# Attention and a wide layer on one core: small products of the identity in the gaps that the planner sees on TensorE

## The chip, the cores and the metric

The kernel runs on one core of one Trainium2 chip. The metric is the device time of one execution in microseconds; less is better. Three runs of the kernel before took 984.73 to 985.93 us, with a median of 985.3 us.

## What is computed

The inputs are q, k and v of shape 8 x 8 x 576 x 64 (batch, heads, positions, head dimension), two weights of 512 x 2048 and 2048 x 512, all float32. The first part is causal attention in a window of 128 positions with a linear bias per head; the second part is a layer on its output, taken as 4608 tokens of 512:

```python
scores = where(0 <= i - j < 128, q @ k.T / 8 - slope[head] * abs(i - j), -1e9)
x = softmax(scores) @ v                      # heads side by side: 4608 x 512
h = x @ w_in
g = h * erf(log1p(exp(h)))
out = g @ w_out
```

## The kernel before, in words

The attention goes in 48 steps of two heads each (`Attention`). A step makes scores on TensorE (L543 for the first eight steps, L614 later), adds the bias on VectorE (L648), takes exponentials on ScalarE (L656), scales by the sums on GpSimd (L679), turns the result (for the first eight steps on TensorE with the identity, L567, copied out by ScalarE or VectorE at L514 and L518; later on VectorE, L696) and multiplies by the values on TensorE (L589, L718). The sums are copied out of PSUM by ScalarE and VectorE (L762, L763, L514, L518).

The layer goes in two passes over the hidden dimension, 7 blocks of 128 and then 9 (`Moe.one_pass`). Each weight and each activation is split into a high and a low part, so each product becomes three. A unit is one block of hidden rows by 384 tokens (512 in the second pass): two halves of six products each (L926, `unit`, one planner operation for each half), a copy of the sums to `hs` by ScalarE (L908) or VectorE (L912), softplus and erf on ScalarE (L963, L965), products and splits on VectorE (L975, L979) and ScalarE, and the products with the second weight (L997). The first pass runs beside the attention. There all units share one PSUM bank for their sums, bank 3 ("h", one buffer): the next unit's first half waits for the copy of the last unit. Columns 0 to 383 hold the sums. The first two attention steps use the whole bank for their turned blocks. In the second pass the units' sums lie in four other banks and are 512 columns wide; a unit whose sums fall into two `hs` buffers is copied in two pieces of 256 columns, each a planner operation of its own that either engine may take.

The weights are read by DMA, put together from two words and split by ScalarE, GpSimd and VectorE (`Weights.prepare`, L802 to L823).

A list scheduler sets the order of the work (`Plan`, L205 on). Every operation has a cost per engine and a due time; `run` (L263) goes through time and gives each engine the ready operation with the earliest due time. It has its own model of TensorE's clock (`on_pe`, L293) and of the delay from one engine to another (`hop`, L219, for example 0.08 + 0.14 + 0.6 = 0.82 us from ScalarE to TensorE). The result is the list `order`, in the order of the decisions; the loop at L366 emits each operation in this order, and each engine runs its own instructions in it. The waits between engines are set from what each emitted instruction reads and writes; all eight banks are one tile, `banks` (L200).

Before the first scores the kernel runs products of a block of zeros (`warm_up`, L478, L485): 22 products of 128 x 128, with the latest due time, so that the planner puts them where TensorE has nothing else to do.

Of the kernel before, what the change touches and what calls it, by code (L numbers as in the profile page):

```python
# [34 lines left out]
ROWS = 0.5  # L35
PLAIN, EARLY = 8, 2
DIRECT = 4
WARM = 22
AHEAD, VA = 4, 13
ND = 3  # L40
# [14 lines left out]
MC, MP, MH = 0.01, 16, -20  # L55
# [155 lines left out]
class Plan:  # L211
# [17 lines left out]
    def op(self, costs, emit, r=(), w=(), at=0.0, moved=0, rows=1.0):  # L229
        o = Op()  # L230
        o.rows = rows
        o.costs, o.emit, o.at, o.seq, o.moved, o.lag = costs, emit, at, len(self.ops), moved, 0.0
        o.outs, o.start, o.engine = [], None, None
        deps, bufs = set(), {}
        for b in r:
            if b.writer:
                deps.add(b.writer)
            b.readers.append(o)
            bufs[id(b)] = b
        for b in w:  # L240
            if b.writer:
                deps.add(b.writer)
            deps.update(b.readers)
            b.writer, b.readers = o, []
            bufs[id(b)] = b
        for b in r:
            if b.writer is o:
                b.readers = []
        for b in [*r, *w]:
            if isinstance(b, Part):  # L250
                bufs[id(b.whole)] = b.whole
        deps.discard(o)
        o.deps, o.bufs = deps, list(bufs.values())
        for b in o.bufs:
            b.users += 1
            if b.users == 1 and b.tag is not None:
                self.slots.setdefault((id(b.pool), b.tag), [b.bufs, []])[1].append(b)
        for d in deps:
            d.outs.append(o)
        self.ops.append(o)  # L260
        return o

    def run(self):  # L263
# [3 lines left out]
        free = {}  # L267
# [51 lines left out]
        while events:  # L319
# [3 lines left out]
            while done and done[0][0] <= t + 1e-9:  # L323
                _, _, o = heapq.heappop(done)
# [38 lines left out]
                    heapq.heappush(events, best.end + best.lag)  # L363
        assert len(order) == len(self.ops), (len(order), len(self.ops))
        self.time = max(o.end for o in order)
        for o in order:  # L366
            self.emit(o)

    def emit(self, o):
# [3 lines left out]
def f32r_us(n):  # L373
    return max(n / 2400.0 + 0.0135, 0.11)
# [6 lines left out]
def dve(n, fast=False):  # L381
    return 0.1 + n * (0.00054 if fast else 0.00108)


def act(n, aps=0, src=0.11):
    return src + 0.093 * aps + n * 0.00084
# [18 lines left out]
def step_time(n):  # L405
    return TE * min(n, NE) + TA * max(0, n - NE)
# [21 lines left out]
class Attention:  # L428
# [49 lines left out]
    def warm_up(self):  # L478
# [4 lines left out]
        op({"DVE": dve(P)}, lambda e: nc.vector.memset(x[:, :P], 0.0), w=[x], at=-30)  # L483
        for _ in range(WARM):
            op({"PE": 0.215}, lambda e: nc.tensor.matmul(  # L485
# [265 lines left out]
    def apply(self, y):  # L751
# [3 lines left out]
        n, c, g, px, at = y.n, y.c, y.g, y.px, y.at + LT  # L755
        if c < DIRECT:
            xs = Part(self.moe.direct(c), slice(None), g, slice(0, CH))
# [70 lines left out]
class Moe:  # L828
# [85 lines left out]
    def unit(self, c, f, w, x, po, start, end, at):  # L914
        nc, op, W = self.nc, self.plan.op, self.width
        U = self.U
        wh, wl = w.t[0, f]
        ps = Buf(self.h_home[0], [P, 512], F32, *self.h_home[1:], f"h{U}")
        for k2 in range(2):
            xh, xl = x[k2]  # L920

            def products(e, k2=k2, xh=xh, xl=xl):
                for k in range(2):
                    cs = slice((2 * k2 + k) * P, (2 * k2 + k + 1) * P)
                    for n, (ww, xx) in enumerate(((wh, xh), (wh, xl), (wl, xh))):
                        nc.tensor.matmul(  # L926
                            ps[:, :W], lhsT=ww[:, cs], rhs=xx[:, k],
                            start=(k2 + k + n == 0), stop=(k2 + k + n == 4),
                        )

            op({"PE": 6 * f32r_us(W) + 0.015}, products, r=[wh, wl, xh, xl], w=[ps], at=at + MH)
        if not self.round:
            self.hs = []
        pos, end_ = len(self.round) * W, (len(self.round) + 1) * W
        base = pos
        while pos < end_:
            i, off = divmod(pos, MW)
            n = min(MW - off, end_ - pos)
            if not off:
                self.hs.append(Buf(self.hp, [P, MW], F32, "m", MB, f"hs{U}_{i}", keep=KH))  # L940
            hs = self.hs[i]
            op({"Act": act(n, src=0.06), "DVE": dve(n)},
               lambda e, hs=hs, off=off, n=n, p0=pos - base: self.copy(e, hs[:, off : off + n], ps[:, p0 : p0 + n]),
               r=[ps], w=[hs], at=at)
            pos += n
        return dict(U=U, c=c, f=f, w=w, po=po, start=start, end=end, at=at)
# [82 lines left out]
@with_exitstack  # L1029
def tile_kernel(ctx, tc, qk, vb, w_in, w_out, plain, bias, out, nb=B):  # L1030
    nc = tc.nc
    nt = nb * S
    nch = nt // CH
    ctx.enter_context(tc.manual_schedule())
    dram = ctx.enter_context(tc.tile_pool(name="dram", bufs=1, space=DRAM))
    const = ctx.enter_context(tc.tile_pool(name="const", bufs=1))
    ident = const.tile([P, P], F32, name="ident")
    nc.scalar.preload_act_table_set(LOG_EXP_SET)
    make_identity(nc, ident)
    x_dram = [Buf(ap=dram.tile([P, NK, CH], F32, name=f"xd{c}")) for c in range(nch)]  # L1040
    part = [Buf(ap=dram.tile([P, DM], F32, name=f"pd{t}")) for t in range(nt // P)]
    plan = Plan()
    w1p = ctx.enter_context(tc.tile_pool(name="w1p", bufs=1))
    stage = ctx.enter_context(tc.tile_pool(name="stage", bufs=1))
    moe = Moe(tc, plan, ctx, x_dram, part, out)
    actx = ctx.enter_context(ExitStack())
    attention = Attention(tc, plan, actx, qk, vb, plain, bias, ident, moe)
    ops = list(plan.ops)


    n1 = nch * NF1
    t0 = LEAD
    t1 = t0 + n1 * TM
    w1 = Weights(nc, plan, lambda k, f: (w1p, f"{k}_{f}"), stage, w_in, w_out, range(NF1), attention.loaded[3:4])
    for k in range(2):
        for f in range(NF1):
            w1.prepare(k, f, t0 - W1A + (f * W1C + W1B * k) * TM)
    accs = [(moe.ps, f"o{t}") for t in range(CH // P)]
    moe.h_home = moe.ps, "h", 1
    moe.one_pass(w1, True, CH, accs, lambda U: t0 + U * TM)  # L1060


    gone, w2p = Buf(ap=True), []

    def close(e):
        actx.close()
        w2p.append(ctx.enter_context(tc.tile_pool(name="w2p", bufs=1)))

    ops += [o for o in plan.ops[len(ops) :] if any(b in o.bufs for b in (moe.raw[1], moe.raw[2]))]
    plan.op({"SP": 0.0}, close, w=[gone], at=0.0).deps.update(ops)  # L1070
    last = plan.ops[-1]
    for o in ops:
        o.outs.append(last)
    pool2 = lambda: w2p[0]
    place = lambda k, f: (
        (pool2, f"{k}_{f}") if f < NF1 + FIT else (w1p, f"{k}_{f - NF1 - FIT}")
    )
    w2 = Weights(nc, plan, place, stage, w_in, w_out, range(NF1, NF))
    tw = step_time(9 * NPAIR * nb // 2)
    for k in range(2):  # L1080
        for f in range(NF1, NF):
            w2.prepare(k, f, tw - W2A + (f - NF1 + (NF - NF1) * k) * W2B, after=[gone])
    moe.h_home = moe.ps, "s", 4
    moe.one_pass(w2, False, CH2, [*accs, (moe.ps, "h")], lambda U: t1 + (U - n1) * TN, pool2, [gone])
    plan.run()
    return plan

# [72 lines left out]
```

## Time and profile before

| | us |
|---|---|
| median of 3 runs (lowest, highest) | 985.3 (984.73, 985.93) |
| the profiled execution | 985.25 |
| its span | 983.3 |
| TensorE busy | 955.2 |
| ScalarE busy | 608.3 |
| VectorE busy | 561.1 |
| GpSimd busy | 149.3 |

The profile is of one execution. Its times are microseconds from the start of the span. PE is TensorE's matmuls, PEld its weight loads, DVE is VectorE, ACT is ScalarE, POOL is GpSimd and SP is SyncE, which issues DMAs. L926 is line 926 of the kernel. A row of instructions names what is written and read (`banks<-xh,whi`). An idle time before an instruction is put down to the work that ended it. The granted clock is the share of TensorE's full clock that the chip granted in a stretch.

### The profile page before, as it was taken

The numbers are of one execution on the slowest core, as the hardware profiler recorded it, in microseconds if no ns is written. First come the engines' busy times: TensorE is split into PE (matmuls) and PEld (weight loads), VectorE is DVE, ScalarE is ACT, GpSimd is POOL, SyncE is SP. The second block draws the span as 40 slices with busy tenths as digits, with TensorE's granted clock in tenths as the row PEclk, the third lists the DMA queues.
The fourth block names the chain that finished last, engine by engine and source line by source line (L and its number), as shares of the span: only waits on it lengthen the run. The fifth ranks groups of instructions, "written<-read, shape, count | busy, mean of one in ns | idle before, by whom it ended". The sixth has DMA issues, their size and how long they took to land.

```text
span 983.3 us, 25856 instructions
## 1 busy us (share of the span) xinstructions
PE 955.2 (97%) x10936; PEld 801.7 (82%) x10936; DVE 561.1 (57%) x1336; ACT 608.3 (62%) x1245; POOL 149.3 (15%) x297
## 2 busy tenths in 40 slices
PE   8788999999999999999999999999999999999997
PEld 6577877888888888989998888888888888888886
DVE  6877885776667666774389434343434343434342
ACT  7878885678667865786688563636363636363552
POOL 3444333333233323000001000000000000000000
PEclk9988999999999999999999999999999999999999
DMA  6675555547555552551034112121212121212021
GB/s 232 217 220 178 171 188 169 184 144 226 180 165 171 184 192 87 199 168 37 33 116 142 64 43 86 43 86 43 87 43 86 43 86 43 86 43 86 1 65 43
DMA packets 52932, 115.09 MB, mean 117 GB/s; under 512 B 5584, under 2 KB 22736, under 8 KB 52816
## 3 DMA queue, kind: packets, MB, share of 16 engines
q1 hardware_dynamic: 52816, 113.43, 36.1%
q8 instruction: 86, 1.41, 0.6%
q14 instruction: 30, 0.25, 0.1%
HBM read 85.10 MB, written 28.31 MB: 115 GB/s over the span
## 4 chain that ended last, share of the span: by engine, by line
PE 81%; ACT 6%; DVE 4%; POOL 3%; DMA 3%; issue 2%; SPq 0%; ACTq 0%; POOLq 0%; DVEq 0%
PE banks L997 37%; PE banks L926 36%; PE banks L718 5%; POOL p L679 3%; PE banks L614 3%; DMA wri<-w_in 2%; ACT p L656 1%; DVE pa L696 1%; ACT s L963 1%; DMA tables<-bias 1%; ACT s L965 1%; ACT L965 1%; ACT L963 1%; ACT L967 0%; ACT wui L809 0%
## 5 line engine op out<-in xcount | busy, mean ns | idle before, releaser
L926 PE MATMUL banks<-xh,whi 128*128 128x384 f32 (+1 forms) x660 | 245.6, 372 | 8.2 <-ACT hs L908 5.5
L926 PE MATMUL banks<-xh,wli 128*128 128x384 f32 (+1 forms) x660 | 240.9, 365 | 1.3 <-DVE wli L823 1.3
L926 PE MATMUL banks<-xl,whi 128*128 128x384 f32 (+1 forms) x660 | 240.7, 365 | 0.0
L997 PE MATMUL banks<-who,gh 128*128 128x512 f32 x576 | 229.6, 399 | 0.5 <-DVE ot L912 0.5
L997 PE MATMUL banks<-wlo,gh 128*128 128x512 f32 x576 | 225.3, 391 | 0.3 <-issue 0.3
L997 PE MATMUL banks<-who,gl 128*128 128x512 f32 x576 | 225.4, 391 | 0.0
L908 ACT COPY hs<-banks 128x384 f32<-128x384 f32 (+2 forms) x127 | 58.4, 468 | 224.0 <-PE banks L926 223.9
L679 POOL TENSOR_SCALAR p<-p,st 128x160 f32<-128x160 f32 (+2 forms) x282 | 139.0, 514 | 228.1 <-DVE st L671 175.4
L926 PEld LDWEIGHTS banks<-xh,whi 128*128 128x128 f32 x660 | 125.1, 190 | 31.1 <-ACT hs L908 7.7
L912 DVE COPY hs<-banks 128x512 f32<-128x512 f32 (+2 forms) x66 | 37.8, 573 | 190.1 <-PE banks L926 170.2
L926 PEld LDWEIGHTS banks<-xl,whi 128*128 128x128 f32 x660 | 125.4, 190 | 15.5
L926 PEld LDWEIGHTS banks<-xh,wli 128*128 128x128 f32 x660 | 125.1, 190 | 14.1 <-DVE wli L823 1.7
L656 ACT ACTIVATE p<-p,st 128x160 f32<-128x160 f32 (+2 forms) x288 | 120.5, 423 | 25.1 <-DVE st L648 23.5
L997 PEld LDWEIGHTS banks<-who,gh 128*128 128x128 f32 x576 | 108.1, 188 | 27.7 <-issue 6.3
L997 PEld LDWEIGHTS banks<-who,gl 128*128 128x128 f32 x576 | 108.1, 188 | 23.5 <-DVE hs L975 0.5
L997 PEld LDWEIGHTS banks<-wlo,gh 128*128 128x128 f32 x576 | 108.1, 188 | 19.3
L975 DVE TENSOR_TENSOR hs<-s,hs 128x768 f32<-128x768 f32 (+1 forms) x106 | 89.9, 884 | 17.3 <-ACT s L965 17.3
L648 DVE CUSTOM_DVE_ANT_0 p<-banks,tables 128x160 f32<-128x160 f32 (+2 forms) x288 | 75.3, 319 | 31.3 <-PE banks L614 30.8
L979 DVE TENSOR_TENSOR gl<-hs,gh 128x768 fp32r<-128x768 f32 (+1 forms) x106 | 91.0, 888 | 0.7
L963 ACT ACTIVATE s<-hs 128x768 f32<-128x768 f32 (+1 forms) x106 | 76.5, 776 | 0.5
L965 ACT ACTIVATE s<-s 128x768 f32<-128x768 f32 (+1 forms) x106 | 76.4, 776 | 0.5
L718 PEld LDWEIGHTS banks<-pa,v 32*64 32x64 f32 x4576 | 59.5, 132 | 14.5 <-issue 8.6
(66 smaller groups left out, 874.5 us busy)
## 6 DMA issues: line engine op xcount, KB each, us to landing
v<-v_b SPq DMA_DIRECT2D x24, 512.0 KB, 4.0
xr<-xd SPq DMA_DIRECT2D x14, 768.0 KB, 4.9
qk<-qk SPq DMA_DIRECT2D x24, 400.0 KB, 4.1
pd<-ot SPq DMA_DIRECT2D x36, 256.0 KB, 3.8
ot<-pd SPq DMA_DIRECT2D x36, 256.0 KB, 3.4
wri<-w_in SPq DMA_DIRECT2D x16, 512.0 KB, 4.2
qk<-qk SPq DMA_DIRECT2D x16, 512.0 KB, 4.6
wro<-w_out SPq DMA_DIRECT2D x16, 512.0 KB, 4.1
```

The source lines that it names most:

```text
L648: nc.vector.tensor_tensor_reduce(out=dst(j), in0=cut(ps[j].all), in1=cut(table[:, half * j + c0 : half * j + c0 + n]), scale=-0.125, scala ...
L656: nc.scalar.activation(dst(j), dst(j), AF.Exp, bias=low[:, j : j + 1], scale=-1.0, accum_out=total[:, j : j + 1])
L679: (nc.vector if e == "DVE" else nc.gpsimd).tensor_scalar(dst, dst, totals[t][:, j : j + 1], 1.0, op0=ALU.mult, op1=ALU.mult)
L718: nc.tensor.matmul(whole[64 * j : 64 * j + 64, first + a, 32 * t0 : 32 * (t0 + n)], lhsT=y.v[rows, 128 * slot + 64 * j : 128 * slot + 64 * ...
L908: self.nc.scalar.copy(out, src)
L912: self.nc.vector.tensor_copy(out, src)
L926: nc.tensor.matmul(ps[:, :W], lhsT=ww[:, cs], rhs=xx[:, k], start=(k2 + k + n == 0), stop=(k2 + k + n == 4),)
L963: A.activation(s[:, :n], hs[:, :n], AF.Softplus)
L965: A.activation(s[:, :n], s[:, :n], AF.Erf)
L975: op({"DVE": dve(n)}, lambda e, s=s, hs=hs, n=n: V.tensor_tensor(hs[:, :n], s[:, :n], hs[:, :n], ALU.mult), r=[s, hs], w=[hs], at=at)
L979: op({"DVE": dve(n)}, lambda e, gh=gh, gl=gl, hs=hs, n=n: V.tensor_tensor(gl[:, :n], hs[:, :n], gh[:, :n], SUB), r=[hs, gh], w=[gl], at=at)
L997: nc.tensor.matmul(po.all, lhsT=gg[:, cs], rhs=w.all, start=(u["start"] and n == 0), stop=(u["end"] and n == 2),)
```

## The change

The planner's loop that emits the operations looks at those of TensorE. If an operation's start in the list lies between 26 and 110 us, if it starts more than 0.3 us after the end of TensorE's operation before it, and if no unit is half done, it first emits int(gap / 0.22) products of the identity with itself, 128 x 128, into columns 384 to 511 of bank 3. A unit is half done between its two halves: the first half's operation is marked open, the second one's not open. Nothing reads those columns in the first pass. The order of all other operations stays as it was.

```diff
+REST = 26, 110
...
         self.time = max(o.end for o in order)
+        free, half = 0.0, False
         for o in order:
+            if o.engine == "PE":
+                if not half and REST[0] < o.start < REST[1] and o.start - free > 0.3:
+                    self.rest(int((o.start - free) / 0.22))
+                free = o.end
+                half = o.open if hasattr(o, "open") else half
             self.emit(o)
...
-            op({"PE": 6 * f32r_us(W) + 0.015}, products, r=[wh, wl, xh, xl], w=[ps], at=at + MH)
+            op({"PE": 6 * f32r_us(W) + 0.015}, products, r=[wh, wl, xh, xl], w=[ps], at=at + MH).open = not k2
...
+    def rest(count):
+        for _ in range(count):
+            nc.tensor.matmul(moe.ps.whole[:, 3, 384:], lhsT=ident[:, :], rhs=ident[:, :], start=True, stop=True)
+
+    plan.rest = rest
     plan.run()
```

## Rows read from the trace of the kernel before

**Rows 1.** The page: the busy time of TensorE with its share and instructions, the granted clock in 40 equal slices of the span (tenths, 9 is 90% or more), and the shares of the chain of waits by engine.
```profile
PE 955.2 (97%) x10936; PEld 801.7 (82%) x10936; DVE 561.1 (57%) x1336; ACT 608.3 (62%) x1245; POOL 149.3 (15%) x297
...
PEclk9988999999999999999999999999999999999999
...
PE 81%; ACT 6%; DVE 4%; POOL 3%; DMA 3%; issue 2%; SPq 0%; ACTq 0%; POOLq 0%; DVEq 0%
```
**Rows 2.** The windows of the trace: for each stretch its start and end, its length, the busy time of TensorE, its weight loads, VectorE, ScalarE and GpSimd, each with its count, then the granted clock, the share of the DMA engines and GB/s.
```profile
31.20:34.90 3.70, 3.28 (x54) 2.94 (x54) 2.12 (x6) 1.21 (x4) 0.76 (x2) 0.55 0.72 268
48.80:55.80 7.00, 6.88 (x89) 5.18 (x90) 4.74 (x17) 4.82 (x15) 4.02 (x8) 0.53 0.63 202
62.20:65.70 3.50, 3.19 (x10) 3.19 (x11) 3.33 (x7) 1.51 (x3) 1.82 (x3) 0.51 0.69 248
79.40:86.10 6.70, 6.09 (x123) 5.59 (x124) 4.28 (x7) 5.09 (x15) 0.00 (x0) 0.50 0.12 31
...
0.00:26.00 26.00, 20.70 (x413) 17.78 (x417) 16.25 (x90) 19.39 (x68) 8.81 (x24) 1.00 0.71 236
26.00:110.00 84.00, 71.76 (x1391) 58.68 (x1391) 68.28 (x211) 66.75 (x183) 33.30 (x57) 0.88 0.61 196
110.00:200.00 90.00, 85.80 (x1867) 71.04 (x1865) 63.81 (x200) 64.04 (x183) 34.30 (x65) 1.00 0.57 179
200.00:983.30 783.30, 776.92 (x7276) 654.18 (x7274) 412.78 (x837) 458.09 (x816) 72.87 (x152) 1.00 0.31 98
```
**Rows 3.** What TensorE waited for between 26 and 110 us: us in total, times, the longest.
```profile
PE banks L926 <- ACT hs L908: 3.2, 3, 2.6
PE banks L926 <- DVE hs L912: 2.7, 1, 2.7
PE banks L567 <- POOL p L679: 2.6, 4, 1.2
PE banks L926 <- DVE wli L823: 1.3, 1, 1.3
...
PE banks L589 <- ACT pa L514: 0.9, 1, 0.9
...
```
**Rows 4.** Pieces of the chain of waits between 44 and 92 us: start, us, what.
```profile
48.92 0.90 PE banks L567 x3
...
53.81 1.86 PE banks L589 x19
...
70.18 0.32 DVE p L648
...
80.01 2.30 PE banks L926 x6
...
87.56 3.00 POOL p L679 x6
```
**Rows 5.** TensorE in order of time: a run of the warm-up's products (start, us, count of records), and unit products at the higher and at the lower clock.
```profile
9.13 2.05 PE L485 MATMUL banks<-warm 128*128 128x128 f32 x16
...
58.04 0.33 PE L926 MATMUL banks<-xh,wli 128*128 128x384 f32 x1
58.21 0.33 PE L926 MATMUL banks<-xh,whi 128*128 128x384 f32 x1
```
**Rows 6.** The second pass: the two copies of one hidden bank in order of time, ScalarE's and VectorE's, and the row of VectorE's waits between 440 and 983 us for this pair (us in total, times, the longest).
```profile
610.80 0.37 ACT L908 COPY hs<-banks 128x256 f32<-128x256 f32 x1 [3.01 <-PE banks L926]
...
611.21 0.42 DVE L912 COPY hs<-banks 128x256 f32<-128x256 f32 x1 [1.08 <-ACT hs L908]
...
DVE hs L912 <- ACT hs L908: 19.8, 17, 2.4
```
**Rows 7.** TensorE in order of time around the gaps; in brackets the idle time before a row and what ended it.
```profile
46.64 0.73 PE L567 MATMUL banks<-ident,p 128*128 128x128 f32 x2 [1.18 <-POOL p L679]
48.09 0.55 PE L567 MATMUL banks<-ident,p 128*128 128x128 f32 x3 [0.71 <-POOL p L679]
48.92 0.90 PE L567 MATMUL banks<-ident,p 128*128 128x128 f32 x3 [0.28 <-POOL p L679]
...
62.51 0.69 PE L926 MATMUL banks<-xh,whi 128*128 128x384 f32 x1 [2.58 <-ACT hs L908]
63.00 0.52 PE L926 MATMUL banks<-xl,whi 128*128 128x384 f32 x1
63.32 0.52 PE L926 MATMUL banks<-xh,wli 128*128 128x384 f32 x1
...
68.94 1.05 PE L614 MATMUL banks<-qk 64*32 64x160 f32 x48
...
73.77 0.44 PE L926 MATMUL banks<-xh,whi 128*128 128x384 f32 x1 [0.48 <-ACT hs L908]
```
**Rows 8.** ScalarE and VectorE in order of time: the copies of bank 3 in or at the end of two of those gaps, VectorE's work ahead of the scores of 68.94 us, and two idle times behind TensorE's work at the low clock.
```profile
48.54 0.49 ACT L908 COPY hs<-banks 128x384 f32<-128x384 f32 x1
...
55.69 0.48 ACT L762 COPY xr<-banks 128x384 f32<-128x384 f32 x1 [1.77 <-PE banks L589]
...
62.00 0.46 ACT L908 COPY hs<-banks 128x384 f32<-128x384 f32 x1
...
69.50 0.69 DVE L816 CUSTOM_DVE_ANT_0 wti<-wti,wui 128x1024 uint16<-128x1024 uint16 x1
...
82.34 0.56 DVE L912 CAST xh<-xr 128x768 fp32r<-128x768 f32 x1 [2.38 <-PE banks L926]
```

## The prediction

> **What bounds the kernel now.** I read the page first [rows 1]: TensorE is busy 97% of the span and the chain of waits is 81% TensorE, while its clock line has low digits only near the start. The windows by stage [rows 2] say where anything is to be had. From 200 us on TensorE is busy 776.92 of 783.3 us at a granted clock of 1.00; from 110 to 200 it lacks 4.2 us. Only the stretch from 26 to 110 us is loose: 71.76 busy of 84 us and a mean clock of 0.88. Four low stretches make that mean: about 31 to 35, 49 to 56, 62 to 66 and 79 to 86 us, at 0.50 to 0.55, which is the lower of the two levels (1.2 instead of 2.4 GHz). The mean puts the lost work at 0.12 x 84 = 10 us of TensorE, an upper end that nobody gets whole.
>
> The list of TensorE's waits in that stretch [rows 3] names what idled it: copies of the hidden sums out of PSUM (hs, ScalarE's L908 3.2 us in 3 waits and VectorE's L912 2.7 us in one), GpSimd's scaling of the softmax (2.6 us in 4) and single waits of 1.3 us and less. Last I read the chain itself [rows 4]. TensorE stands on it at a low clock in two places alone, 48.92 to 55.67 us and 80.01 to 82.31 us; the first low stretch lies beside a chain on other engines, and between 55.7 and 80 us the chain is GpSimd, VectorE and ScalarE. So a better clock is worth far less than 10 us.
>
> **What the change does.** It moves no existing operation and no DMA; queues of SP and GpSimd are passed by nothing. It puts int(gap / 0.22) products of 128 x 128 ahead of each TensorE operation (of one list time between 26 and 110 us) before which the planner's list sees more than 0.3 us idle, except between the two halves of one hidden unit. They write columns 384 to 511 of bank 3. Columns 0 to 383 of that bank are the hidden unit's sums, which ScalarE or VectorE copies out. The warm-up issues 22 such products and its rows show 44 records, two to a product; they give the price [rows 5]: 16 records, 8 products, in 2.05 us, so 0.24 us each with the tail off; at the low clock twice that at most, and the unit's own products went from 0.175 us start to start to 0.32 us, so I take 0.24 x 0.32 / 0.175 = 0.44 us.
>
> **Do they run inside the gap?** That decides the sign. A wait on a copy of bank 3 is harmless only if waits are kept by columns. The kernel before has a place that shows it: in its second pass one hidden bank is copied in two pieces of 256 columns, one by ScalarE and one by VectorE, which depend on the same products and on nothing of each other. ScalarE's runs from 610.80 to 611.17, and VectorE, idle for 1.08 us, starts its piece at 611.21. The waits count 17 of these, 19.8 us [rows 6]. Two readers of different columns in one bank are thus kept one behind the other. I take the same for a product that writes the bank.
>
> The Trainium skill, "PSUM — Partial Sum Buffer", section "PSUM bank collisions raise a hardware error", asks for this: guard by bank and quadrant, not by address, TensorE's writes against ScalarE's or VectorE's reads included, disjoint columns too. No run here shows a collision; the waits between two readers agree with it. By the page the sum is the one that follows, by addresses alone it is the first rival's.
>
> So a filler waits for every copy of bank 3 that the list put ahead of it. Ahead of the first half of a unit the copy always comes first, since that half is waiting for it. There the fillers leave the gap idle, start when the unit could have started, and push it back. The gaps seen by the list are not in a trace; I use the chip's; the list's may be smaller, down to none, or longer, by up to the 0.82 us that its own code (L219) adds from ScalarE to TensorE.
>
> **The sum, gap by gap** [rows 3, 4, 7, 8].
> (a) Before 45 us: single waits, the longest 1.3 and 0.9 us [rows 3]. No copy of bank 3 stands ahead or it is long done; some 10 fillers run inside. The chain there waits for a DMA and works on VectorE and ScalarE. 0; if a few overrun, the 0.5 us of two of them.
> (b) 45.4 to 48.9 us, the transposes that wait for GpSimd (1.18, 0.71, 0.28). ScalarE's copy of the unit runs at 48.54, between the releases at 48.09 and 48.92, so the rows don't say which the list puts first. If the fillers come first, 8 to 12 fit and the stretch to 55.67 runs at full speed: worth 1.8 us, because ScalarE idled only 1.77 before the copy at 55.69. If the copy comes first, 12 fillers begin at 49.0: 7 at 0.44 and 5 at 0.24 are 4.3 us, transposes end 54.4 instead of 49.8, and the work behind them, 3.3 us at full speed instead of 5.9, ends at 57.7 instead of 55.6: plus 2.1. The copy lies midway between the releases, so I take 0 and keep -1.8 and +2.1.
> (c) 59.94 to 62.51 us, ahead of a unit, 2.58 us: 11 fillers after the copy that ends at 62.46. The idle stays, so the clock still falls; low for about 3.1 us as before, 7 fillers at 0.44, then 4 at 0.24: 4.1 us. Of the unit's products behind them the nine that fitted into the low stretch at 0.32 now go at 0.175 and give back 1.3: plus 2.8. L718 and the scores L614 (68.94) go with it, and VectorE's L648 at 70.18, which starts 0.2 us behind those scores, opens the next part of the chain.
> (d) 77.25 to 80.01 us, ahead of a unit, 2.7 us: 12 fillers, 7 at 0.44 and 5 at 0.24 are 4.3 us, then six products in 1.3 us: the end moves from 82.31 to 85.6, plus 3.3. VectorE sat idle 2.38 us for these products (xh at 82.34), and behind that cast the chain is VectorE and from 87.56 GpSimd: all of it is moved.
> (e) Small waits ahead of units: 0.48 us at 73.77 is 2 fillers, 0.5 us; others of 0.2 us are under the limit unless the list adds its own delay. Between 0 and 2.9 us (eight further unit starts by one or two fillers, 0.36 us each); I take 0.5, from the one row.
> Together 0 + 0 + 2.8 + 3.3 + 0.5 = 6.6 us. From 110 us on nothing takes it back: the waits there are on the same chain, and TensorE is full afterwards. The profiled execution took 985.25 us, its span 983.3, the median of the three runs is 985.3, so the sum stands on either: 991.9 us. The likeliest case's own range is 988 to 996.4, the upper end with (b) at 2.1 and (e) at 2.9, the lower with (b) at -1.8 and two thirds of the fillers of (c) and (d). The copies of later units wait for the fillers ahead of them too, which lie on TensorE ahead of those units' products anyway: nothing.
>
> **Rivals.** First, faster: a filler waits for nothing, either because writes are guarded by columns or because the list issues its fillers ahead of the copies. Place and price: (b) gives 1.8 us; (c) nearly nothing, as VectorE's L648 at 70.18 follows directly on its own L816, which starts at 69.50 [rows 8], 0 to 0.7; (d) 1.0 us, the 2.30 us of [rows 4] against 1.3. Together 2.8 to 3.5: 982.2 us. It decides if the fillers start at the beginning of (c) and (d). For it speaks that warm-up products in the gaps before 26 us went with a clock of 1.00 [rows 2]; against it [rows 6]. Second, nothing much: the list sees few of these gaps, or places fillers mostly where the chain is elsewhere, (a); within 2 us of before. The planner models waits but not this chip's exact ones. Third, worse: (b) falls badly and the list sees longer gaps than the chip, 11 us and more: 996.4 us and up.
>
> **How the numbers follow.** A measurement of this kernel tells from no change about 0.2%, 2.0 us. Fillers behind the copies: 0.56; worse still: 0.09; little: 0.13; inside the gaps: 0.22. The last two give same 0.13 and faster 0.22, the first two slower 0.65. The likeliest gives 991.9 us. The range 982.4 to 996.4 cuts about 0.12 below, half of the fast case, and 0.08 above.
>
> **What would show it.** In the changed profile the new products appear at the end of the waits at about 62.5 and 80, not in them, with a wait on the copies L908 and L912 of their own; the unit behind them starts 4 us later; the clock still falls in the low stretches at 62 and 79 us. I am wrong if the fillers start at 60 and 77 us and the mean clock of 26 to 110 us rises to 0.95 or more with the chain shorter. (b) is read from whether fillers stand before or after the copy at 48.5. If some 20 products or fewer are there, it was the second rival.

## The result, and the profile after

The changed kernel took 991.24 us (median of 17 runs, 986.36 to 993.98), the kernel before beside it 984.84 us (median of 17). The ratio is 1.0062, interval 1.0050 to 1.0073: slower by 6.1 us, against the 6.6 us of the sum. The profiled execution took 993.63 us, 2.4 us over the median, with a span of 991.8 us. On a second occasion (`e_after_again` below) the ratio was 1.0065, interval 1.0039 to 1.0091.

The page of the changed kernel: busy time, granted clock, and the chain by line. Lines from 367 on are 7 to 13 higher than before; L933 is the old L926, L915 and L919 the old L908 and L912, L725, L621 and L574 the old L718, L614 and L567, L1095 the new products.
```profile
PE 966.5 (97%) x11044; PEld 813.6 (82%) x11044; DVE 561.1 (57%) x1336; ACT 607.7 (61%) x1245; POOL 149.4 (15%) x297
...
PEclk9999989999999999999999999999999999999999
...
PE banks L1004 36%; PE banks L933 36%; PE banks L725 5%; PE banks L621 3%; POOL p L686 2%; ACT p L663 2%; DMA wri<-w_in 2%; PE banks L1095 1%; ACT s L970 1%; DVE p L655 1%; DMA tables<-bias 1%; ACT s L972 1%; ACT L972 1%; ACT L970 1%; DVE pa L703 0%
```
TensorE has 108 records more, which are 54 products, and its clock line is better than in [rows 1]; yet the new line L1095 stands in the chain of what ended last. TensorE in order of time says where the products went (start, us, records; idle time before and what ended it), with the work that follows three of them:
```profile
27.60 0.71 PE L1095 MATMUL banks<-ident 128*128 128x128 f32 x4
...
29.28 2.27 PE L1095 MATMUL banks<-ident 128*128 128x128 f32 x18
...
45.34 2.17 PE L1095 MATMUL banks<-ident 128*128 128x128 f32 x18
...
52.70 1.09 PE L574 MATMUL banks<-ident,p 128*128 128x128 f32 x8
...
60.13 4.39 PE L1095 MATMUL banks<-ident 128*128 128x128 f32 x24 [3.08 <-ACT hs L915]
64.18 0.67 PE L933 MATMUL banks<-xh,whi 128*128 128x384 f32 x1
...
66.72 1.53 PE L725 MATMUL banks<-pa,v 32*64 32x96 f32 x112
...
71.58 1.05 PE L1095 MATMUL banks<-ident 128*128 128x128 f32 x8
...
80.49 4.28 PE L1095 MATMUL banks<-ident 128*128 128x128 f32 x24 [2.07 <-DVE hs L919]
...
90.70 1.16 PE L1095 MATMUL banks<-ident 128*128 128x128 f32 x8 [0.93 <-ACT hs L915]
...
95.87 0.60 PE L1095 MATMUL banks<-ident 128*128 128x128 f32 x4
```
The two groups of 12 sit behind the waits of [rows 7], not in them: TensorE is idle for 3.08 and 2.07 us (2.58 and 2.67 before), the copy ends, then the products run for 4.4 and 4.3 us, and only then comes the unit. The group at 45.34 is the other kind: it fills the wait for GpSimd. ScalarE and VectorE show the copies that the products wait for, and the cast that waits for the second unit:
```profile
59.62 0.46 ACT L915 COPY hs<-banks 128x384 f32<-128x384 f32 x1
...
79.91 0.52 DVE L919 COPY hs<-banks 128x384 f32<-128x384 f32 x1
...
86.13 0.56 DVE L919 CAST xh<-xr 128x768 fp32r<-128x768 f32 x1 [5.70 <-PE banks L933]
```
VectorE's idle time before that cast has grown from 2.38 us [rows 8] to 5.70. The windows, in the columns of [rows 2]:
```profile
26.00:110.00 84.00, 74.47 (x1444) 64.78 (x1442) 66.39 (x206) 63.59 (x178) 33.34 (x58) 0.96 0.61 190
110.00:200.00 90.00, 87.29 (x1810) 71.72 (x1800) 63.42 (x197) 63.52 (x178) 33.18 (x61) 0.96 0.59 179
60.10:64.50 4.40, 4.37 (x25) 4.37 (x26) 4.16 (x8) 1.35 (x2) 2.88 (x5) 0.64 0.43 163
80.40:84.80 4.40, 4.31 (x25) 4.32 (x26) 0.03 (x1) 3.03 (x7) 0.00 (x0) 0.66 0.00 1
129.00:137.00 8.00, 8.00 (x176) 5.99 (x176) 5.22 (x15) 4.00 (x13) 3.87 (x6) 0.57 0.48 134
```
The clock of 26 to 110 us rose from 0.88 to 0.96, but within both late groups it is still low. A new low stretch stands at 129 to 137 us, where the kernel before had 1.00 from 110 to 200.

Where the 8.5 us between the two spans lie: the products of 60.13 begin 2.4 us before the unit of [rows 7] did at 62.51, behind the filled wait at 45 (how much of this is that wait's, see (b) below); L725 behind the unit is 0.5 us late (66.72 against 66.23, its start before); the cast is 3.8 us late (86.13 against 82.34). The rest, 4.7 us, comes later. VectorE runs the same 1336 instructions in the same order in both kernels, so they can be matched one by one: they are 3.7 us late at 120 us of the kernel before, 6.1 at 145, behind the new low stretch, 4.5 at 220, and 8.4 from 447 us to the end. So the delay is not fixed at 110 us; it falls and grows in pieces that I did not follow.

### The profile page after: what moved, and what is told of

Its sections match the earlier page's. It is cut to its first block, busy times and chain, and to the rows that moved or that the text cites. A ratio compares the mean times of both kernels' runs of the same rounds, so it can differ in the third digit from the quotient of the medians.

```text
span 991.8 us, 26072 instructions
## 1 busy us (share of the span) xinstructions
PE 966.5 (97%) x11044; PEld 813.6 (82%) x11044; DVE 561.1 (57%) x1336; ACT 607.7 (61%) x1245; POOL 149.4 (15%) x297
## 4 chain that ended last, share of the span: by engine, by line
PE 82%; ACT 7%; DVE 4%; DMA 3%; POOL 2%; issue 2%; SPq 0%; ACTq 0%; POOLq 0%; DVEq 0%
PE banks L1004 36%; PE banks L933 36%; PE banks L725 5%; PE banks L621 3%; POOL p L686 2%; ACT p L663 2%; DMA wri<-w_in 2%; PE banks L1095 1%; ACT s L970 1%; DVE p L655 1%; DMA tables<-bias 1%; ACT s L972 1%; ACT L972 1%; ACT L970 1%; DVE pa L703 0%
## 5 line engine op out<-in xcount | busy, mean ns | idle before, releaser
L933 PE MATMUL banks<-xh,whi 128*128 128x384 f32 (+1 forms) x660 | 244.3, 370 | 2.9 <-ACT hs L915 2.8
L933 PE MATMUL banks<-xh,wli 128*128 128x384 f32 (+1 forms) x660 | 239.5, 363 | 0.0
L933 PE MATMUL banks<-xl,whi 128*128 128x384 f32 (+1 forms) x660 | 239.4, 363 | 0.0
L915 ACT COPY hs<-banks 128x384 f32<-128x384 f32 (+2 forms) x127 | 58.4, 468 | 225.1 <-PE banks L933 225.0
L919 DVE COPY hs<-banks 128x512 f32<-128x512 f32 (+2 forms) x66 | 37.8, 573 | 190.2 <-PE banks L933 170.2
L933 PEld LDWEIGHTS banks<-xh,whi 128*128 128x128 f32 x660 | 124.1, 188 | 25.0 <-ACT hs L915 5.3
L933 PEld LDWEIGHTS banks<-xl,whi 128*128 128x128 f32 x660 | 124.3, 188 | 15.4
L933 PEld LDWEIGHTS banks<-xh,wli 128*128 128x128 f32 x660 | 124.2, 188 | 12.6
L725 PEld LDWEIGHTS banks<-pa,v 32*64 32x64 f32 x4576 | 59.3, 132 | 14.1 <-issue 8.5
```

Of the source, the lines that this page charges most:

```text
L725: nc.tensor.matmul(whole[64 * j : 64 * j + 64, first + a, 32 * t0 : 32 * (t0 + n)], lhsT=y.v[rows, 128 * slot + 64 * j : 128 * slot + 64 * ...
L915: self.nc.scalar.copy(out, src)
L919: self.nc.vector.tensor_copy(out, src)
L933: nc.tensor.matmul(ps[:, :W], lhsT=ww[:, cs], rhs=xx[:, k], start=(k2 + k + n == 0), stop=(k2 + k + n == 4),)
```

## The experiments

My theory: a filler (one of the added products) waits for every earlier copy out of its bank, so the groups ahead of a unit run behind the copy, on the path. The rivals: the products cost by their number, wherever they are; or the loss is that of the clock later on. All ratios are to the kernel before in the same comparison.

**Another bank.** The list says which of the four score banks nobody holds at that moment; the products go there, in the same places.
```diff
-                    self.rest(int((o.start - free) / 0.22))
+                    bank = min(idle, key=lambda k: idle[k])   # last user emitted longest ago
+                    self.rest(int((o.start - free) / 0.22), bank)
...
-            nc.tensor.matmul(moe.ps.whole[:, 3, 384:], ...
+            nc.tensor.matmul(moe.ps.whole[:, bank, :P], ...
```


> The same 54 products in the same places of the list, but written to columns 0 to 127 of one of the four score banks that the list holds empty at that moment, instead of to bank 3. Theory (a product waits for every earlier copy out of its bank, so those ahead of a unit run behind the copy and only push the unit back): the products start right behind the work before them, near 57 and 75 us, instead of at 60.13 and 80.49; no wait of theirs on L915 or L919 is left; VectorE's cast that stood at 82.34 us before and 86.13 after comes at 80 to 82; time 981 to 984 us, 1 to 3.5 us under the kernel before. Rival (the products themselves, or the low clock from 129 to 137 us in the changed profile, cost the time, and not the wait): 989 to 992 us, as the change.

983.36 us against 983.54, ratio 1.0003 (0.9983 to 1.0022). The loss is gone. TensorE in order of time, and the window from 26 to 110 us (here L1106 is the new products, L944 the unit and L926 ScalarE's copy):
```profile
56.20 2.94 PE L1106 MATMUL banks<-ident 128*128 128x128 f32 x24
59.33 0.45 PE L944 MATMUL banks<-xh,whi 128*128 128x384 f32 x1 [0.19 <-ACT hs L926]
...
74.14 2.84 PE L1106 MATMUL banks<-ident 128*128 128x128 f32 x24
76.86 0.44 PE L944 MATMUL banks<-xh,whi 128*128 128x384 f32 x1
```
```profile
26.00:110.00 84.00, 79.39 (x1520) 68.00 (x1519) 71.55 (x224) 70.75 (x196) 35.97 (x63) 1.00 0.64 207
```
The same 12 products now run inside the wait, at full clock, and the unit is held up by 0.19 us or nothing. VectorE's cast comes at 78.21, earlier than the 80 to 82 expected. That is the theory against the rival by number. But the expected gain of 1 to 3.5 us is not seen (the interval allows 1.7 at most), although the clock is 1.00 from 26 to 110 us.

**The same bank, ahead of the copy.** Each group is emitted right behind the operation at which its gap begins; the copy then comes after it.
```diff
-                    self.rest(int((o.start - free) / 0.22))
+                    ahead[id(last)] = int((o.start - free) / 0.22)
...
             self.emit(o)
+            if id(o) in ahead:
+                self.rest(ahead[id(o)])
```


> The same 54 products in bank 3, but emitted right behind the TensorE operation at which the gap begins, so ahead of the copy out of that bank and not behind it; the copy now waits for the products. Theory (order against the copy decides): the products start near 56 and 74 us with no wait on L915 or L919, the copies that ScalarE and VectorE make at the end of the gaps are not held, as they came 2 us later anyway; time as with the empty score bank, within 0.2% of the kernel before. Rival (bank 3 itself is the matter, whatever the order, as products and copies then hinder each other the other way round): 3 us or more above the kernel before.

984.7 us against 984.27, ratio 1.0001 (0.9985 to 1.0017).
```profile
54.62 2.94 PE L1098 MATMUL banks<-ident 128*128 128x128 f32 x24
...
72.56 2.84 PE L1098 MATMUL banks<-ident 128*128 128x128 f32 x24
```
```profile
57.61 0.48 ACT L918 COPY hs<-banks 128x384 f32<-128x384 f32 x1 [0.27 <-PE banks L1098]
...
75.44 0.56 DVE L922 COPY hs<-banks 128x384 f32<-128x384 f32 x1 [0.68 <-PE banks L1098]
```
No wait for a copy stands before either group. Now the copies wait for the products (L1098), 0.27 and 0.68 us, although I had expected them not to be held: the wait goes by the bank in this direction too. The loss is gone without another bank. So it is the order against the copy of the same bank that costs.

**Parts of the set.** `e_no_unit` leaves out the 30 products ahead of a unit after 50 us, `e_unit_only` has only these, and `e_double` has 24 where the change has 12.
```diff
-if not half and REST[0] < o.start < REST[1] and o.start - free > 0.3:
+if ... and not (o.start > 50 and hasattr(o, "open")):     # e_no_unit
+if ... and o.start > 50 and hasattr(o, "open"):           # e_unit_only
...
+self.rest(n * (2 if n == 12 else 1))                      # e_double
```


> The change without the 30 products ahead of a unit's first half after 50 us (12, 12, 4 and 2); the 24 others stay in bank 3. Theory: no product stands behind a copy that its unit waits for; what is left is the gain at 49 to 56 us, 1.8 to 2.9 us: 982 to 984 us. Rival (any added product costs, as TensorE is the bound): 54 products cost 6.4 us, so 24 cost 2.8 us: 987.6 us.

983.77 us, ratio 1.0008 (0.9992 to 1.0024): the interval holds no change, and leaves out both the theory's gain (1.8 us would be 0.9982) and the rival's 2.8 us (1.0028). So these 24 products cost nothing to be seen, and the gain did not come.

> The change with the 30 products ahead of a unit's first half after 50 us alone (12, 12, 4 and 2). Theory: the loss without the gain at 49 to 56 us: 2.8 + 3.3 + 0.5 to 1.5 us, 991.5 to 993 us, above the change. Rival (cost by number of products): 30 of 54 of 6.4 us, 3.6 us: 988.4 us, below the change.

994.01 us, ratio 1.0113 (1.0090 to 1.0136): the loss, and more of it than in the change, as the theory has it against the rival by number; but 11 us instead of 7 to 8.

> The change with the two groups of 12 products ahead of a unit doubled to 24 each, 78 products in all. Theory (they run behind the copy, all on the path): the first 7 of each group run at the low clock, the 24 more at 0.24 us: 5.8 us more than the change, 997 us. Rival (they fill idle time and only the overrun costs, or the cost lies at 129 to 137 us): 1 to 3 us more, 992 to 994 us.

995.12 us, ratio 1.0127 (1.0095 to 1.0159). Against the change's 1.0062 that is 6.4 us for 24 more products, near the theory's 5.8. (It is under the expected 997 because the kernel before was faster beside it, 983.54 us, than beside the change.) In its profile the second group of 24 takes 5.62 us without a fall of the clock, where 12 took 4.28 at a low one.

**The two large terms alone.** REST = 50, 60 leaves the 12 products of term (c), REST = 66, 75 those of (d).

> Of the change only the 12 products ahead of the unit that started at 62.51 us before (term c of the prediction), in bank 3. Theory (behind the copy, all on the path): plus 2.8 us against the kernel before, 2.5 to 3.5. Rival (the loss is that of the whole set, through the clock later on): within 1 us of the kernel before.

986.79 us, ratio 1.0024 (1.0007 to 1.0040): plus 2.4 us, just under the expected 2.5.

> Of the change only the 12 products ahead of the unit that started at 80.01 us before (term d of the prediction), in bank 3. Theory: plus 3.3 us against the kernel before, 2.8 to 4. Rival: within 1 us of the kernel before.

987.26 us, ratio 1.0030 (1.0013 to 1.0048): plus 3.0 us. Both terms are there, and both intervals hold the predicted size. Then both together, and the 30 and the change once more, these three on one chip (the two single terms had been measured on another):
```diff
+if ... and 50 < o.start < 75 and hasattr(o, "open"):      # e_cd
```


> Of the change only the two groups of 12 products ahead of units (terms c and d together), in bank 3. If the terms add: 2.4 + 3.0, measured alone, 5.4 us above the kernel before, 0.55%. If they don't (as the 11 us of all 30 products ahead of units suggest): 8 us and more.

995.6 us against 984.19, ratio 1.0125 (1.0109 to 1.0141, 4 runs): plus 12.3 us, not 5.4.

> The 30 products ahead of units once more, which took 11.1 us more than the kernel before in 6 runs. If the terms add: 5.4 us and 6 x 0.24 us, 6.8 us above the kernel before, and the 11.1 was the chance of those runs; if it is a cost of its own: 9 us and more again.

996.33 us, ratio 1.0124 (1.0106 to 1.0142): plus 12.2 us. So the 11.1 was not the chance of the first six runs. It is also no more than (c) and (d) without the 6 other products took.

> The change itself on the same chip as the two others. If the terms add, it lies near the 30 products alone, less at most 1.8 us for the stretch at 49 to 56 us: 5 to 7 us above the kernel before; if not, several us below the 30 alone.

991.32 us, ratio 1.0065 (1.0039 to 1.0091), 5 us below the 30 alone. The terms don't add. A piece of the excess stands in the traces: group (d) of `e_d_only`, then groups (c) and (d) of `e_cd`.
```profile
76.14 2.94 PE L1095 MATMUL banks<-ident 128*128 128x128 f32 x24 [2.55 <-DVE hs L919]
```
```profile
60.70 2.94 PE L1095 MATMUL banks<-ident 128*128 128x128 f32 x24 [2.58 <-ACT hs L915]
...
79.48 4.57 PE L1095 MATMUL banks<-ident 128*128 128x128 f32 x24 [2.71 <-DVE hs L919]
```
Alone, group (d) took 2.94 us at a granted clock of 1.00; behind group (c) it took 4.57 us at 0.63, and 4.50 and 4.57 us in `e_unit_only` and `e_unit_again`. That is 1.6 us of the 6.9 by which the two together exceed the sum of the two alone. Why the clock falls there only with (c) in place is not shown. More comes behind 110 us: against the kernel before, VectorE's matched instructions lose another 4.2 to 7.4 us in the three executions with both groups and without the 24 other products, none and 2.3 us in those with one group; but 5.5 us in that of `e_trim` (below), a version that lost nothing. One such piece is a stop of TensorE in `e_unit_only` around 229 us, far behind the last filler:
```profile
229.03 1.79 PE L621 MATMUL banks<-qk 64*32 64x160 f32 x40 [2.56 <-issue]
```
In the middle of the scores of one step, 8 of 48 records in, TensorE stood for 2.56 us for no work that the profile names, and the clock fell behind it. `e_cd` has such a stop of 1.69 us at 229.23, but `e_d_only` has one of 2.25 us at 225.50 and `e_no_unit`, which lost nothing, one of 1.73 us at 221.74; the kernel before has none there. So the stop doesn't tell the versions with the excess from the others. The cause of the rest of the excess stays open.

The stops have one thing in common that their rows don't say. Behind 110 us the 13 traces have 24 of them over 0.5 us, and each ends 1.2 to 1.6 us after a 16 KB packet of the instruction queue (q8 on the page) has landed; these packets start at least 3.3 us apart there. That looks like TensorE waiting for its own instructions; no run tests it.

**Without the overrun.** REST = 26, 75 in the version with another bank drops the last two groups.

> The products in an empty score bank, without the last two groups (4 and 2 products), which had no idle time on the chip behind them: 48 products. Theory (what the empty bank left over was their overrun, 6 x 0.24 us): 1 to 2 us under the version with all 54 and as much under the kernel before, 0.1 to 0.2%. Rival: the gain of the clock is not on the path, no difference to the kernel before.

983.17 us against 984.27, ratio 1.0004 (0.9985 to 1.0023): the medians lie as expected, but the interval holds no difference, as the rival has it; the overrun is not shown to cost anything. In its profiled execution the low stretch that the changed kernel had at 129 us is back, without any filler behind a copy:
```profile
121.00:129.00 8.00, 8.00 (x176) 5.90 (x175) 5.73 (x17) 3.79 (x12) 3.86 (x6) 0.57 0.48 139
```
So that stretch alone does not make the loss: this version has it and loses nothing.

## Why the prediction was right

**The wait** was the step that decided, and it held. The two copies of [rows 6] gave away that waits go by bank; the products ahead of a unit started behind the copy, at 60.13 and 80.49 us. The other bank and the other order each took away the loss. The Trainium skill's page "PSUM — Partial Sum Buffer" and the runs agree in what they show of order; no run shows a collision. One sign that I had named for being wrong came true all the same: the mean clock of 26 to 110 us rose to 0.96. The chain did not get shorter with it.

**(a)** 11 products ran before 45 us, where I foresaw some 10, beside the chain: nothing, as `e_no_unit` bears out.

**(b)** The fillers came ahead of the copy: 9 products in 2.17 us. From the last unit product before them to the transposes at 52.70 it takes 7.54 us; in the profiled execution of the kernel before it took 10.45, so the two profiles give 2.9 us, more than the 1.8 that I had bounded it with. But `e_c_only`, `e_d_only` and `e_unit_only`, which have no products there either, took 8.82 to 9.08 us: there 1.3 to 1.5 us are left to win. The medians of `e_no_unit` give none of it (1.0008), so it is not in the time, and where it goes stays open. My 0 was the middle between a gain and a loss; that it came out is luck.

**(c)** 12 products instead of 11. From their start to L725 it takes 6.59 us, from the unit's start to L725 it took 3.72: plus 2.9, predicted 2.8; alone 2.4. It doesn't need the low clock that I worked it out with: in `e_c_only` the group ran at full clock in 2.94 us, 4.99 to L725, against 2.31 from the unit's start in `e_d_only`: plus 2.7.

**(d)** From the start of the products to the cast 5.64 us, before from the unit's start 2.33: plus 3.3, as predicted; alone 3.0, with the group at full clock.

**(e)** Two more groups ahead of units, 4 and 2 products, between my 2 and my upper end; one group of 4 at 71.58 us ahead of L725 I had not foreseen. The 0.5 us is not seen: `e_unit_again` with the 4 and 2 products (12.2 us) and `e_cd` without them (12.3) take the same.

**What was wrong** is the sum as a sum. (c) and (d) together measure 12.3 us, not 5.4, and the rest of the set takes 5 to 6 us of it back although alone it gains nothing. I had also put the work behind 110 us at nothing; in the profiled execution 4.7 of the 8.5 us lie there. That 6.6 forecast meets 6.1 measured is in part luck.

**The first rival's price** was wrong too. Fillers in the gap gave 0, not 2.8 to 3.5 us. One reason is that I took the four low stretches of one execution for a property of the kernel. `e_d_only` shows the unit of (c) behind the same wait as in [rows 7], its window and its first products:
```profile
58.70:62.00 3.30, 3.25 (x90) 3.00 (x93) 3.16 (x7) 1.28 (x3) 1.88 (x3) 1.00 0.62 230
```
```profile
58.75 0.44 PE L933 MATMUL banks<-xh,whi 128*128 128x384 f32 x1 [2.58 <-ACT hs L915]
59.03 0.34 PE L933 MATMUL banks<-xl,whi 128*128 128x384 f32 x1
```
2.58 us idle, as in the kernel before, and no fall of the clock: 0.34 us a product instead of 0.52. Over 23 runs of the kernel before, the mean clock lay between 0.988 and 0.996 and the time between 979 and 988 us; the profiled one was at 0.988, the bottom. In most executions there was less to win than [rows 2] showed.

That is not the whole of it. The price came from (b) and (d) almost alone, and these stretches are low again in the other traces without products there: (b) in `e_c_only`, `e_d_only` and `e_unit_only`, (d) in `e_c_only` and `e_no_unit`, where L725 behind the unit took 2.13 and 2.14 us instead of 1.53. And over the runs of `e_free_bank` the mean clock was 0.997, that of the kernel before beside it 0.993: 0.004 of 983 us is 4 us of clock, and none of it is in the time. Where it went is not shown.

## What to carry to other kernels

Work that is meant to fill idle time must not wait for what the idle time waits for: before filling a gap on TensorE, look whether the bank that the filler writes has a copy queued ahead, by any columns, and put the filler into a bank that nobody holds or ahead of the copy. A pair of instructions in the old profile that share a bank and nothing else tells how the waits go. And a clock line of one execution is one draw: the gain of holding the clock is to be priced over several executions' clocks, not from the profiled one, and a higher mean clock is not yet time. Nor do the prices of single groups add up: measure the set, not only its parts.

## What the runs showed of the hardware

The same wait of 2.58 us was followed by the lower clock in one execution (products of 0.52 us) and by the full one in another (0.34 us). One piece of the work had a clock of 1.00 in the kernel before (125 to 133 us there) and 0.57 in two other executions (129 to 137 us in the changed kernel, 121 to 129 us in `e_trim`), with fillers behind the copy and without. Twelve products behind a copy took 2.94 us at a clock of 1.00 in one version and 4.57 us at 0.63 in another, with the same idle time ahead of them within 0.2 us (2.55 and 2.71). And 54 products more raised the granted clock of 26 to 110 us to 1.00 where they filled the gaps, without a measurable gain in time. TensorE stopped 24 times for more than 0.5 us without a named wait behind 110 us in 13 traces, each time until 1.2 to 1.6 us after a packet of the instruction queue.
